# Sparse attention with an expert layer on one Trainium2 core: sixteen tiles normalised inside the turn, and a planner that counts TensorE's activity over a sliding stretch

## The chip, the cores and the metric

The kernel runs on one core of a Trainium2 chip. The metric is device time in microseconds (us). The kernel before takes 828.85 us, the median of 3 runs (826.21 to 830.17). The engines are named as the profile names them: PE is TensorE's matmul, PEld its weight load, DVE is VectorE, ACT is ScalarE, POOL is GpSimd, SP is the engine that issues most DMAs.

## The reference

```python
def _attn_ref(q, k, v):                    # (4, 8, 576, 64) each, float32
    scores = scale * np.matmul(q, k.transpose(0, 1, 3, 2))
    kth = np.partition(scores, -32, axis=-1)[..., -32:-31]
    scores = np.where(scores >= kth, scores, -1000000000.0)
    attn = np.exp(scores - np.max(scores, axis=-1, keepdims=True))
    attn = attn / (np.sum(attn, axis=-1, keepdims=True) + 1e-09)
    return np.matmul(attn, v)

def _moe_ref(x, w_a, w_b, w_out):          # x: (2304, 512), d_ff 1536
    return (x @ w_a) * (x @ w_b) @ w_out
```

Every row of attention keeps its 32 largest scores; the heads of a token are laid side by side and go through the expert layer. All is float32.

## The kernel before, in words

**The tiles.** The work is cut into 8 chunks of 256 or 320 tokens. A chunk has 4 pairs of heads, and a pair has 4 or 5 tiles: a tile is 64 query rows of both heads of a pair (128 partitions) against 576 keys. There are 144 tiles; tiles 0 to 15 are chunk 0, tiles 16 to 35 chunk 1. For each tile: `scores` (L456, TensorE) fills a PSUM tile; `topk` copies half of it out (L469 or L467, ACT), folds it into a minimum and a maximum half (L476, L478, DVE) and finds the 32nd largest score with four rounds of max8 and match_replace (L484, L486, DVE), with POOL making the exponent's bias (L489) for the first 36 tiles; `softmax` masks and exponentiates into P with the row's sum beside it. The first 35 tiles do this on TensorE and ACT: L520 (ACT) makes a mask, L525 (TensorE) adds it to the scores, L527 (ACT) is the exponential. Then L530 (POOL) adds 1e-9 to the sum, L533 (DVE) takes its reciprocal into `sm[:, 1:2]`, and L537 (POOL) multiplies the tile's P, 128x576, by it. `transpose` turns P in five blocks of 128x128 with TensorE transposes against an identity (L559), four into one PSUM tile `mm` and the fifth into another for the first 30 tiles, and ACT copies both out (L561). When all tiles of a pair are turned, `av` (L589) multiplies by V, and ACT and POOL split the result into a high and a low part (L599 to L601).

**The experts.** Weights come as float32 words and are converted into two fp32r parts by `convert` (L406 to L415: four ACT, one or two DVE and two POOL operations of 128x512 per weight, 36 weights, in the first 200 us), while attention of chunks 0 and 1 goes on. `up` (L627 to L629) and `down` (L661 to L663) are three fp32r products per block. For the first two chunks `up` also copies a second PSUM tile into the SBUF tile `b` (L648), and `down` copies its result into `b` before the store (L668). `b` has one buffer.

**The order of the work.** No engine's order is written by hand. Every operation is entered into `Plan` with an engine, a modelled cost, a key, what it reads and writes, and the buffers it needs. `Plan.order` then runs a model of the engines in time: a free engine takes the operation with the smallest key that is ready and whose buffers are free (a tag's buffers are taken in the order of the program; `mm` alone is free of that). The kernel is emitted in that order, and on the chip each engine works through its list strictly in order. Scores and top-k of tile i have the key -1000 + i, a tile's turn the key i, a chunk's experts 1000 and more, so that a turn gives way to later tiles' scores and goes ahead of the experts.

**TensorE's clock in the planner.** The model doubles the cost of a PE operation when the count of columns that ended in the last period of length `TICK` is under `BUSY`. Where PE has nothing for over `FILL_SLACK`, and the count of the present period is under `FILL_COLUMNS`, the planner puts in a filler: a bf16 product of 256 columns into an `mm` tile that nobody reads (L316). There are two `mm` buffers, shared by fillers, turned blocks of the first 30 tiles, one step of the first 24 conversions, `av`, `up` and `down`.

**DMA in the planner.** A load is modelled as landing 0.85 us after its bytes have passed; operations that read it are ready from then.

Of the kernel before, what the change touches and what calls it, by code (L numbers as in the profile page):

```python
# [8 lines left out]
FT = mybir.dt.float32  # L9
# [6 lines left out]
OP = mybir.AluOpType  # L16
# [9 lines left out]
KEEP = 1  # L26
APART = 24
FILL_SLACK = 0.15
XF_BUFS = 1
P_BUFS, JOINT = 2, 8  # L30
LAG = 0
# [7 lines left out]
MASKS = "P" * 35 + "QV" * 55  # L39
SCALAR_SCALE = 50  # L40
POOL_PRODUCT = 2
CONV_FIRST = 14
CONV_BIG = 4
CONV_AWAY = (0, 2, 4, 6, 8, 10, 11)
# [51 lines left out]
class Plan:  # L96
# [46 lines left out]
    def order(self):  # L143
        ops = self.ops
        n = len(ops)
        wait = [len(o.deps) for o in ops]
        outs = [[] for _ in ops]
        for k, o in enumerate(ops):
            for d in o.deps:
                outs[d].append(k)  # L150
        ready = [0.0] * n
        place = [0] * n
        for r, k in enumerate(sorted(range(n), key=lambda k: (ops[k].key, k))):
            place[k] = r
        held, head = {t: 0 for t in self.rings}, {t: 0 for t in self.rings}
        heaps, free = {e: [] for e in self.GAP}, {e: 0.0 for e in self.GAP}
        cols, events, drops, parked, taken, order = {}, [], [], {}, set(), []
        dma = hw = now = port = 0.0
        for k in range(n):
            if not wait[k]:  # L160
                heapq.heappush(heaps[ops[k].engine], (place[k], k))

        def wake(t):
            for r, k in parked.pop(t, ()):
                heapq.heappush(heaps[ops[k].engine], (r, k))

        def full(k):
            need = {}
            for b in ops[k].bufs:
                if b not in taken:  # L170
                    need.setdefault(b.tag, []).append(b)
            for t, bs in need.items():
                h = head[t]
                if held[t] + len(bs) > bs[0].bufs or t not in self.LOOSE and self.rings[t][h:h + len(bs)] != bs:
                    return t

        left, products = n, sum(o.engine == "PE" for o in ops)

        def fill():
            b = self.filler[0]()  # L180
            self.rings["mm"].append(b)
            b.left, b.first = 1, "PE"
            ops.append(Op("PE", self.filler[1], 0, lambda: self.filler[2](b), (), [b], 1, False, 0.65, False))
            outs.append([])
            return len(ops) - 1

        while left:
            started = False
            for e, h in heaps.items():
                if free[e] > now + self.EPS:  # L190
                    continue
                aside, pick = [], None
                while h:
                    r, k = heapq.heappop(h)
                    if ready[k] > now + self.EPS:
                        aside.append((r, k))
                        continue
                    t = full(k)
                    if t is None:
                        pick = k  # L200
                        break
                    parked.setdefault(t, []).append((r, k))
                for x in aside:
                    heapq.heappush(h, x)
                soon = min((ready[k] for _, k in aside), default=1e9)
                if pick is not None:
                    left -= 1
                    products -= e == "PE"
                elif (e == "PE" and products and now > FILL_FROM and now + FILL_SLACK < soon and held["mm"] < 2
                        and cols.get(int(now / self.TICK), 0) < FILL_COLUMNS):  # L210
                    pick = fill()
                else:
                    continue
                started = True
                order.append(pick)
                o = ops[pick]
                for b in o.bufs:
                    if b not in taken:
                        taken.add(b)
                        held[b.tag] += 1  # L220
                        head[b.tag] += 1
                        wake(b.tag)
                if e == "SP":
                    free[e] = now + 0.05 * o.num
                    hw = max(hw, now) + (0.625 if o.inner else 0.45) * o.num
                    dma = max(dma, hw + 0.65) + o.cost
                    end = dma + 0.85
                elif e == "PE":
                    slow = cols.get(int(now / self.TICK) - 1, 0) < self.BUSY
                    end = free[e] = now + o.cost * (2 if slow else 1)  # L230
                    tick = int(end / self.TICK)
                    cols[tick] = cols.get(tick, 0) + o.cost * 2400 * o.rows
                else:
                    end = now + o.cost
                    if o.port:
                        port = end = max(end, free["POOL"] + o.cost - self.SHARED)
                    elif e == "POOL":
                        end = max(end, port + o.cost - self.LOCKED)
                    free[e] = end
                heapq.heappush(events, (end, pick))  # L240
                heapq.heappush(events, (free[e], -1))
            if started:
                continue
            now = events[0][0]
            while drops and drops[0][0] <= now + self.EPS:
                t = heapq.heappop(drops)[1]
                held[t] -= 1
                wake(t)
            while events and events[0][0] <= now + self.EPS:
                end, k = heapq.heappop(events)  # L250
                if k < 0:
                    continue
                e = ops[k].engine
                for b in ops[k].bufs:
                    b.left -= 1
                    if not b.left:
                        at = end + (0 if e == b.first else self.HOP.get((e, b.first), 0.2))
                        heapq.heappush(drops, (at, b.tag))
                        heapq.heappush(events, (at, -1))
                for d in outs[k]:  # L260
                    wait[d] -= 1
                    to = ops[d].engine
                    ready[d] = max(ready[d], end + (self.GAP[e] if e == to else self.HOP.get((e, to), 0.2)))
                    if not wait[d]:
                        heapq.heappush(heaps[to], (place[d], d))
                        heapq.heappush(events, (ready[d], -1))
        self.length = now
        return order
# [10 lines left out]
def attn_moe(ctx: ExitStack, tc, qT, kT, kW, v, wa, wb, wo, out):  # L279
# [38 lines left out]
    def buf(shape, dtype, tag, bufs, pool=work):  # L318
        return Buf(pool, shape, dtype, tag, bufs)
# [179 lines left out]
    def softmax(i, s, found):  # L499
# [31 lines left out]
        else:  # L531
            act(1, lambda: nc.scalar.activation(sm[:, 1:2], sm[:, 0:1], AF.Copy, bias=1e-9), [], [sm], k=URGENT)
        dve(1, lambda: vec.reciprocal(sm[:, 1:2], sm[:, 1:2]), [], [sm])  # L533
        if i >= SCALAR_SCALE and i % 2 == 0:
            act(S, lambda: nc.scalar.activation(pt.ap, pt.ap, AF.Copy, scale=sm[:, 1:2]), [sm], [(both, w)], ptr=1)
        else:
            pool(0, lambda: nc.gpsimd.tensor_scalar(pt.ap, pt.ap, sm[:, 1:2], 1.0, op0=OP.mult, op1=OP.mult), [sm], [(both, w)], 0.81)  # L537
        return both

    PT = {}  # L540

    def transpose(i, both):
        t = tiles[i]
# [4 lines left out]
        for n, m in ((0, 4), (4, 5)) if i < FRONT else ((0, last),):  # L548
            tp = mm_tile() if i < FRONT else buf([128, 2, 512], FT, "tp", 1, psum)

            def at(tp=tp, n=n, m=m):
                x = tp.ap if i < FRONT else tp.ap.rearrange("p a b -> p (a b)")
                return x[:, 0:128 * (m - n)].rearrange("p (k q) -> p k q", q=128)

            def turn(at=at, n=n, m=m):
                pf = both.ap.rearrange("p w a b -> p (w a b)")
                of = [(640 if t["joint"] else S) * w + 128 * kb for kb in range(4)] + [512 if t["joint"] else S * w + 448]
                for kb in range(n, m):
                    nc.tensor.transpose(at()[:, kb - n, :], pf[:, of[kb]:of[kb] + 128], ident)  # L559
            pe((m - n) * 262, turn, [(both, w)] + ([(both, 0)] if t["joint"] and w else []), [tp])  # L560
            act(128 * (m - n), lambda at=at, n=n, m=m: nc.scalar.activation(  # L561
                turned[:, n:m, :, t["off"]:t["off"] + 64], at().rearrange("p k (h q) -> p k h q", h=2), AF.Copy),
                [tp], [(turned, t["s"], n)], ps=True, k=URGENT if i < FRONT and HURRY else None)
# [315 lines left out]
```

## Time and profile before

| | |
|---|---|
| median of 3 runs | 828.85 us |
| the profiled execution | 829.44 us |
| its span, first to last instruction | 827.7 us |
| mean granted clock of TensorE | 0.973 |
| busy share PE, DVE, ACT, POOL | 94%, 82%, 71%, 50% |

The profile is of one execution. The median is 0.6 us under its time, and 1.7 us of its time lie around the span. Busy shares are means over stages with different limits. PE's busy time counts fillers too, and modelled ends of pipelined matmuls, so a busy PE is not a useful one. The granted clock has two levels here, 1.2 GHz (0.5 in the profile's figures) and 2.4 GHz (1.0); a share between them is a mix of both over the stretch.

### The profile page before, as it was taken

The page shows a single profiled execution, that of the slowest core. Times are in us where ns is not written, and L with a number is a line of the kernel's source. Part 1 is how long each engine was busy: PE and PEld are TensorE (multiplying, and loading weights), DVE is VectorE, ACT ScalarE, POOL GpSimd, SP SyncE. Part 2 cuts the span into 40 slices and gives each one's busy share as a digit, 9 for nine tenths or more (in the row PEclk, how much of TensorE's full clock was granted, in tenths as well). Part 3 has the DMA queues.
Part 4 walks back from the last instruction along what each step waited for, and adds up shares of the span by engine and source line. Part 5 has one row for each costly group of instructions (what it writes and reads, how often), then busy time and mean ns, then how long its engine had stood idle before and what let it go on. Part 6 is the DMA issues. An engine that isn't in the chain of part 4 may idle for free. (4 is left out here: it accounts for less than half of the span.)

```text
span 827.7 us, 17219 instructions
## 1 busy us (share of the span) xinstructions
PE 782.1 (94%) x5736; PEld 611.0 (74%) x5736; DVE 680.7 (82%) x2239; ACT 584.2 (71%) x1348; POOL 412.6 (50%) x581
## 2 busy tenths in 40 slices
PE   5787879889999999999999999999999999999997
PEld 2333356765688876888778877887788878898995
DVE  6888998596999999999999999999999999960110
ACT  5888998997678777777677777777677767851220
POOL 3776887898376743444334443443344434440120
PEclk7788999989999999999999999999999999999999
DMA  7766767775277723776338834784367436650660
GB/s 259 270 233 238 252 227 247 284 249 172 71 219 249 237 91 113 260 253 213 101 109 272 294 139 143 273 294 127 128 227 259 155 105 223 215 199 26 208 238 29
DMA packets 76383, 163.46 MB, mean 197 GB/s; under 512 B 5888, under 2 KB 37632, under 8 KB 76288
## 3 DMA queue, kind: packets, MB, share of 16 engines
q1 hardware_dynamic: 76016, 162.03, 58.3%
q8 instruction: 48, 0.79, 0.4%
q14 instruction: 47, 0.39, 0.1%
q10 hardware_dynamic: 272, 0.26, 0.1%
HBM read 144.97 MB, written 17.30 MB: 196 GB/s over the span
## 5 line engine op out<-in xcount | busy, mean ns | idle before, releaser
L627 PE MATMUL mm<-xh,w 128*128 128x256 f32 (+1 forms) x768 | 240.5, 313 | 3.0 <-ACT pt L561 2.0
L629 PE MATMUL mm<-xh,w 128*128 128x256 f32 (+1 forms) x768 | 227.9, 297 | 0.0
L628 PE MATMUL mm<-xl,w 128*128 128x256 f32 (+1 forms) x768 | 227.9, 297 | 0.0
L484 DVE MAX8 top<-mx 128x8 f32<-128x296 f32 x432 | 186.7, 455 | 0.9
L627 PEld LDWEIGHTS mm<-xh,w 128*128 128x128 f32 x768 | 145.8, 190 | 19.4 <-issue 10.8
L628 PEld LDWEIGHTS mm<-xl,w 128*128 128x128 f32 x768 | 146.5, 191 | 0.3
L629 PEld LDWEIGHTS mm<-xh,w 128*128 128x128 f32 x768 | 145.8, 190 | 0.0
L651 POOL TENSOR_TENSOR gl<-a,gh 128x256 fp32r<-128x256 f32 (+1 forms) x96 | 79.3, 826 | 112.9 <-ACT gh L650 104.0
L486 DVE MATCH_REPLACE8 mx<-top,mx 128x296 f32<-128x296 f32 x288 | 128.6, 450 | 0.0
L510 POOL TENSOR_TENSOR p<-sb,p 128x576 f32<-128x576 f32 x55 | 78.2, 1422 | 73.8 <-ACT p L509 72.6
L561 ACT ACTIVATE pt<-tp 128x512 f32<-128x512 f32 (+1 forms) x114 | 74.6, 655 | 52.8 <-PE tp L559 51.7
L537 POOL TENSOR_SCALAR p<-p,sm 128x576 f32<-128x576 f32 x97 | 73.4, 757 | 63.1 <-DVE sm L533 63.0
L645 DVE SCALAR_TENSOR_TENSOR a<-mm,a 128x320 f32<-128x320 f32 (+1 forms) x72 | 32.9, 457 | 72.2 <-PE mm L629 68.2
L661 PE MATMUL mm<-wo,gh 128*128 128x512 f32 x216 | 89.0, 412 | 0.4 <-ACT pt L561 0.4
L663 PE MATMUL mm<-wo,gl 128*128 128x512 f32 x216 | 84.7, 392 | 0.0
L662 PE MATMUL mm<-wo,gh 128*128 128x512 f32 x216 | 84.5, 391 | 0.0
L589 PE MATMUL mm<-pt,vr 128*64 128x256 f32 (+1 forms) x544 | 77.1, 430 | 1.3 <-ACT pt L561 1.2
L559 PE MATMUL tp<-ident,p 128*128 128x128 f32 x522 | 77.6, 276 | 0.4 <-POOL p L537 0.4
L559 PEld LDWEIGHTS tp<-ident,p 128*128 128x128 f32 x522 | 60.2, 140 | 19.1 <-ACT bias L491 6.6
L650 ACT ACTIVATE gh<-a 128x256 fp32r<-128x256 f32 (+1 forms) x96 | 42.3, 441 | 41.9 <-DVE a L645 38.3
L476 DVE TENSOR_TENSOR mn<-s,sb 128x288 f32<-128x288 f32 x134 | 59.2, 445 | 14.2 <-ACT sb L469 12.6
L467 ACT ACTIVATE sb<-s 128x576 f32<-128x576 f32 x109 | 69.1, 635 | 1.2 <-PE s L456 1.2
(105 smaller groups left out, 1526.0 us busy)
## 6 DMA issues: line engine op xcount, KB each, us to landing
w<-wd SPq DMA_DIRECT2D x168, 512.0 KB, 4.4
wd<-w SPq DMA_DIRECT2D x24, 512.0 KB, 3.9
kr<-kT SPq DMA_DIRECT2D x32, 288.0 KB, 3.3
vr<-v SPq DMA_DIRECT2D x24, 384.0 KB, 3.6
kw<-kW SPq DMA_DIRECT2D x24, 288.0 KB, 3.6
wo<-wa SPq DMA_DIRECT2D x12, 512.0 KB, 5.9
qr<-qT SPq DMA_DIRECT2D x16, 320.0 KB, 5.0
wo<-wb SPq DMA_DIRECT2D x9, 512.0 KB, 5.3
```

The lines of the kernel that those rows point to most:

```text
L484: dve(HS + 8, lambda r=r: vec.max(eight(r), mx[:, g]), [(mx, g, 0), (mx, g, 1)], [tk[r]], 0.393)
L486: dve(HS + 8, lambda r=r: vec.match_replace(mx[:, g], eight(r), mx[:, g], LOW), [tk[r]], [(mx, g, 0), (mx, g, 1)], 0.453)
L510: pool(S, lambda: nc.gpsimd.tensor_tensor(pt.ap, sb.ap, pt.ap, OP.subtract), [sb], [(both, w)])
L559: nc.tensor.transpose(at()[:, kb - n, :], pf[:, of[kb]:of[kb] + 128], ident)
L589: mm(ps[e, :n], vr[:, (kb + 1) % 5, e], turned[:, kb, h, :n], start=(kb == 0), stop=(kb == 4))
L627: mm(ps[:, :n], w[:, 0, kb, :], xh[:, kb, :n], start=(kb == 0), stop=False)
L628: mm(ps[:, :n], w[:, 0, kb, :], xl[:, kb, :n], start=False, stop=False)
L629: mm(ps[:, :n], w[:, 1, kb, :], xh[:, kb, :n], start=False, stop=(kb == 3))
L651: pool(n, lambda: nc.gpsimd.tensor_tensor(gl[:, j, on], a[:, :n], gh[:, j, on].bitcast(FT), OP.subtract), [a, (gh, j)], [(gl, j)])
L661: mm(ps.ap, gh[:, j, on], fin[j][:, 0], start=(j == turn[c][0]), stop=False)
L662: mm(ps.ap, gh[:, j, on], fin[j][:, 1], start=False, stop=False)
L663: mm(ps.ap, gl[:, j, on], fin[j][:, 0], start=False, stop=(j == turn[c][-1]))
```

## The change

For tiles 0 to 15 the product of P with its rows' reciprocals leaves POOL. POOL instead scales the 128x128 identity by the reciprocals into a diagonal matrix (same instruction, 128 columns in place of 576), and each of the five blocks of P is turned by an ordinary float32 product with that diagonal in place of a transpose. The diagonal lies in a buffer of the tag `b`, of which there is one, so that the next tile's diagonal can be written only when the five blocks of the tile before have been turned.

The planner changes in three places. It counts columns over the last `TICK` before the present moment, in place of fixed periods, with the columns of an operation spread over its time. A filler is put in if that count is under `FILL_COLUMNS` where PE has nothing for `FILL_SLACK`, and also, where something becomes ready sooner, if the count is under `FILL_HOT`. A DMA is modelled as landing 1.5 us after its bytes have passed. So the emitted order can differ everywhere, on every engine and in the DMA queue.

```diff
+FILL_HOT = 4000
+LANDING = 1.5
+DIAGONAL = 16
@@ Plan.order
-        cols, events, drops, parked, taken, order = {}, [], [], {}, set(), []
+        recent, events, drops, parked, taken, order = [], [], [], {}, set(), []
+        def active():
+            while recent and recent[0][1] < now - self.TICK:
+                recent.pop(0)
+            return sum((end - max(start, now - self.TICK)) * rate for start, end, rate in recent)
-                elif (e == "PE" and products and now > FILL_FROM and now + FILL_SLACK < soon and held["mm"] < 2
-                        and cols.get(int(now / self.TICK), 0) < FILL_COLUMNS):
+                elif (e == "PE" and products and now > FILL_FROM and held["mm"] < 2
+                        and active() < (FILL_COLUMNS if now + FILL_SLACK < soon else FILL_HOT)):
                     pick = fill()
-                    end = dma + 0.85
+                    end = dma + LANDING
                 elif e == "PE":
-                    slow = cols.get(int(now / self.TICK) - 1, 0) < self.BUSY
-                    end = free[e] = now + o.cost * (2 if slow else 1)
-                    tick = int(end / self.TICK)
-                    cols[tick] = cols.get(tick, 0) + o.cost * 2400 * o.rows
+                    times = 2 if active() < self.BUSY else 1
+                    end = free[e] = now + o.cost * times
+                    recent.append((now, end, 2400 * o.rows / times))
@@ softmax
-        if i >= SCALAR_SCALE and i % 2 == 0:
+        if i < DIAGONAL:
+            one = diagonal[i] = buf([128, 512], FT, "b", 1)
+            pool(0, lambda: nc.gpsimd.tensor_scalar(one[:, 0:128], ident, sm[:, 1:2], 1.0, op0=OP.mult, op1=OP.mult), [sm], [one], 0.27)
+        elif i >= SCALAR_SCALE and i % 2 == 0:
@@ transpose
-                    nc.tensor.transpose(at()[:, kb - n, :], pf[:, of[kb]:of[kb] + 128], ident)
-            pe((m - n) * 262, turn, [(both, w)] + ([(both, 0)] if t["joint"] and w else []), [tp])
+                    if i < DIAGONAL:
+                        mm(at()[:, kb - n, :], pf[:, of[kb]:of[kb] + 128], diagonal[i][:, 0:128], start=True, stop=True)
+                    else:
+                        nc.tensor.transpose(at()[:, kb - n, :], pf[:, of[kb]:of[kb] + 128], ident)
+            pe((m - n) * (520 if i < DIAGONAL else 262), turn, [(both, w)] + ([(both, 0)] if t["joint"] and w else [])
+               + ([diagonal[i]] if i < DIAGONAL else []), [tp])
```

## Rows read from the trace of the kernel before

**Rows 1.** Busy time of each engine in four stretches, with granted clock and DMA share.

```profile
core 0: us, PE busy (x) PEld busy (x) DVE busy (x) ACT busy (x) POOL busy (x), PEclk, DMA share, GB/s
0.00:108.00 108.00, 80.72 (x478) 36.93 (x478) 88.39 (x274) 90.14 (x192) 73.06 (x107) 0.84 0.72 250
108.00:195.00 87.00, 76.40 (x555) 55.78 (x554) 69.59 (x209) 80.82 (x186) 74.40 (x105) 0.94 0.69 245
195.00:740.00 545.00, 543.22 (x4188) 444.89 (x4188) 516.81 (x1743) 397.76 (x937) 253.83 (x355) 1.00 0.58 191
740.00:828.00 88.00, 81.77 (x520) 73.39 (x518) 5.88 (x14) 15.48 (x35) 11.30 (x15) 0.99 0.35 124
```

**Rows 2.** What ACT waited for in 0 to 108: us in total, times, longest.

```profile
ACT wo L406 <- DMA wo<-wa: 3.9, 2, 2.5
ACT xf L599 <- PE mm L589: 3.4, 2, 1.8
ACT sb L469 <- PE s L456: 3.0, 1, 3.0
ACT pt L561 <- PE mm L559: 2.5, 4, 0.8
...
ACT mm L410 <- PE mm L316: 0.8, 2, 0.7
```

**Rows 3.** What DVE waited for in 0 to 108, the rows that name POOL.

```profile
DVE wo L412 <- POOL bias L489: 2.4, 1, 2.4
DVE sm L533 <- POOL sm L530: 1.5, 2, 1.2
```

**Rows 4.** Groups by line in 0 to 108: busy us, mean ns | idle before.

```profile
L316 PE MATMUL mm<-ident,nident 128*128 128x256 bf16 x132 | 31.8, 295 | 4.9 <-ACT pt L561 1.8 <-DVE wo L412 0.4
...
L559 PE MATMUL mm<-ident,p 128*128 128x128 f32 x80 | 16.2, 314 | 9.8 <-ACT pt L561 5.4 <-POOL sm L530 1.4 <-POOL p L537 0.7
L589 PE MATMUL mm<-pt,vr 128*64 128x256 f32 x80 | 13.6, 506 | 0.5 <-ACT pt L561 0.4
...
L537 POOL TENSOR_SCALAR p<-p,sm 128x576 f32<-128x576 f32 x16 | 12.0, 748 | 2.0 <-DVE sm L533 2.0
...
L489 POOL TENSOR_SCALAR bias<-t 128x1 f32<-128x1 f32 x18 | 3.8, 214 | 7.7 <-DVE t L484 7.2
...
L424 POOL TENSOR_SCALAR_AFFINE_SELECT ident<-ident 128x128 f32<-128x128 f32 x1 | 0.3, 292 | 0.1
```

**Rows 5.** Timeline of PE: turned blocks and one `av` at half and at full clock.

```profile
60.91 1.09 PE L559 MATMUL mm<-ident,p 128*128 128x128 f32 x4
...
63.52 4.53 PE L589 MATMUL mm<-pt,vr 128*64 128x256 f32 x20 [0.37 <-ACT pt L561]
...
91.54 0.74 PE L559 MATMUL mm<-ident,p 128*128 128x128 f32 x5 [0.29 <-ACT xf L599]
...
105.69 2.38 PE L589 MATMUL mm<-pt,vr 128*64 128x256 f32 x20
```

**Rows 6.** Busy time and granted clock inside the first 108 us, columns as in rows 1.

```profile
20.00:39.00 19.00, 14.47 (x78) 6.04 (x76) 16.43 (x48) 16.43 (x35) 14.87 (x21) 0.77 0.77 254
39.00:59.00 20.00, 15.86 (x98) 8.02 (x98) 15.39 (x48) 17.85 (x41) 14.91 (x22) 0.84 0.70 252
59.00:80.00 21.00, 16.82 (x98) 7.61 (x91) 18.09 (x61) 17.40 (x39) 15.03 (x23) 0.76 0.64 221
80.00:108.00 28.00, 22.61 (x160) 11.03 (x159) 26.39 (x84) 27.35 (x61) 21.36 (x31) 1.00 0.74 259
```

**Rows 7.** Timelines: tile 3's reciprocal, tile 2's fifth block; tile 6's, tile 5's.

```profile
36.13 0.15 DVE L533 RECIPROCAL sm<-sm 128x1 f32<-128x1 f32 x1
...
37.01 0.30 PE L559 MATMUL mm<-ident,p 128*128 128x128 f32 x1 [0.47 <-DVE gl L412]
...
54.73 0.15 DVE L533 RECIPROCAL sm<-sm 128x1 f32<-128x1 f32 x1
...
55.90 0.33 PE L559 MATMUL mm<-ident,p 128*128 128x128 f32 x1 [0.69 <-ACT pt L561]
```

More of the change, by code (lines that the diff above doesn't have):

```diff
@@ L538, in softmax @@
         return both
-    PT = {}
+    PT, diagonal = {}, {}
     def transpose(i, both):
```

## The prediction

> **What bounds the kernel now.** I read four views, from the whole to the part. First the busy time by stage [rows 1]. From 195 to 740 us PE is busy 543.2 of 545 us, and DVE 516.8; after that PE alone works off what is left. So from 195 us on the end is set by PE's remaining work, which the change leaves as it is: every tile from 16 on is turned as before, and no expert product changes. Before 195 us PE is not the bound. In 0 to 108, the time of chunk 0's attention, it is idle 27.3 us, and 31.8 us of its busy time are 132 fillers that nobody reads [rows 1, 4]. There the fullest engines are ACT (90.1 of 108) and DVE (88.4); POOL has 73.1. In 108 to 195 ACT has 80.8 of 87. All that the change adds or removes lies in the first 108 us, and chunk 0's experts and all later tiles stand behind it. So what the front gains or loses moves the end by about the same, and what does not reach ACT or DVE there costs nothing.
>
> Second, what these two wait for [rows 2, 3]. In 0 to 108 ACT waited 6.7 us for PE after its first tile (3.4 + 2.5 + 0.8), 3.9 for weights, and for POOL in no row; DVE waited 3.9 for POOL (2.4 + 1.5). Third, the groups of that stretch [rows 4] give the prices, and fourth the timeline [rows 5] the same PE work at both clock levels.
>
> The profiled execution took 829.4 us (span 827.7 and 1.7 around it), 0.6 over the median of 828.85; the sum is made against 829.4. A measurement of this kernel can tell about 0.5% from no change, 4.1 us, so "the same" is 824.7 to 833.0.
>
> **POOL's scaling goes.** It was 16 x 748 ns = 12.0 us [rows 4]. The diagonal is the same instruction on 128 columns. Between the same kind on 1 column (214 ns) and on 576 (748 ns) a line gives 214 + 127 x 534/575 = 332 ns; the nearest row of its very shape, another operation, has 292. I take 332: 16 x 332 = 5.3 us, and POOL has 6.7 us less to do. The ends are 7.3 us (at 292) and 0 (at 748). Little of this reaches the end. ACT waits for POOL in no row, and DVE for 3.9 us in two [rows 2, 3]. The rest of POOL's time is covered by ACT's and DVE's own work; without that cover the whole 6.7 would count. I take -1.0 us, as POOL's queue gets 9% shorter and the conversions ahead of those two small operations stay; ends -3.9 and 0.
>
> **The turn gets dearer on TensorE.** 80 transposes become 80 float32 products. The trace shows what a float32 product is: the four `av` of chunk 0 have 40 such products, and 80 matmuls stand in the row of L589 [rows 4], so two passes each. A pass of 256 columns at full clock in `av` takes about 2.38/20 = 0.12 us, with two running side by side in the array's halves; a turned block of 128 columns takes 1 pass, and five take 0.74 with a modelled end of the last near 0.27, so (0.74 - 0.27)/4 = 0.12 each. At half clock four take 1.09, the last near 0.47: 0.21 each [rows 5]. So I add one pass of 0.12 to 0.21 us per block, 9.4 us at full clock and 16.6 at half. The 27.3 idle us and the fillers of PE take it in. What is not covered is a delay in order: PE works through its list in order, so scores and masks behind a turn come 0.6 to 1.0 us later, and ACT's copies too. That counts only where ACT has nothing else, and ACT is idle 17.9 of 108 us [rows 1], 17%: 0.17 x 9.4 = +1.6 us. Ends 0 and +9.4 (each of the delays met in full, at full clock). Per tile POOL's part of the chain from reciprocal to turned block is 0.42 us shorter and PE's 0.6 longer, about even, so no gain is expected there.
>
> One rule speaks against the change. The Trainium skill (TensorE: Matmul & The Clock Gate, Terms) says that the transpose mode is 4 times faster for float32. By that, as an estimate, the 80 products would cost three more passes each, 28 us at full clock, and by the same 17% +4.8 us in place of +1.6, which would make the sum 829.5. The trace shows a factor of two: two passes where the transpose has one, of the same columns.
>
> **The clock.** From 20 to 80 us the granted clock is 0.77, 0.84 and 0.76 [rows 6], a mix of the two levels; 2 x (0.23 x 19 + 0.16 x 20 + 0.24 x 21) = 25 us of these 60 ran at 1.2 GHz. From 80 to 108 it is 1.00. In the slower stretches PE is busy 76 to 80% of the time, in the full one 81%; the shares lie too near each other to say from them what a few more fillers do. The change puts fillers in more evenly and more often, and the products are twice the columns in the turns. If the half clock went away, PE's work in ACT's 6.7 us of waits would halve, as `av` does (4.53 to 2.38): -3.4. I take half of that, -1.7. The ends are -3.4 and +3.4, for a plan whose fillers fall elsewhere and lose the full stretch too.
>
> **DMA and the new order.** Nothing is loaded more or less. The later modelled landing puts readers of weights further back in ACT's, PE's and POOL's lists, so that ACT meets fewer loads still under way; it waited 3.9 us for two [rows 2]. I take half, -2.0; ends -3.9 and +3.9, where a load has long landed and its reader stands behind other work. SP's list is planned by the same model, with the same transfers. The order as a whole is new from the first operation. That this is worth anything by itself no row shows; it gets 0, with the 6.2 us in which ACT was idle in 108 to 195 [rows 1] as its bound on either side.
>
> **The sum:** -1.0 + 1.6 - 1.7 - 2.0 = -3.1; 829.4 - 3.1 = 826.3, say **826.3 us**. All four terms at their better ends give -11.2 (818), at their worse +16.7 (846); the likeliest case by itself, with the terms about half out each way, is 822 to 833.
>
> **Rival 1: a front that runs at full clock and meets its loads (faster).** The fillers hold the clock from 20 us on and loads are met on time. ACT's waits for PE (6.7) and for weights (3.9) nearly vanish, 10.6, with DVE's 1.0 for POOL, less 1.6 for the longer turns: -10, so 819 us; half of it, 824, is already faster. For it: 25 us at half clock, in a stretch that holds nearly all fillers. Against it: 132 fillers did not hold it there, and ACT, busy 83% already, has own work to put in place of many waits. The Trainium skill (TensorE: Matmul & The Clock Gate, Part 4: PE-mode transpose) holds that transposes do not count as activity for the clock; by that rule the products of the change would count where the transposes did not. No row separates transposes from the rest: they are spread through the slow and the full stretches alike.
>
> **Rival 2: the one buffer of the diagonal (slower).** Tile i+1's diagonal may be written only when tile i's fifth block is turned, and that block waits in turn for one of two `mm` tiles. In the trace tile 3's reciprocal is there at 36.13 + 0.15, but tile 2's fifth block ends at 37.31; tile 6's at 54.88, tile 5's block at 56.23 [rows 7]. That is 1.0 and 1.4 us, and the five blocks now take 0.6 to 1.0 longer: about 2 us. If POOL stands at the diagonal in the order of its list, behind it wait the conversions' sums, the bias and the row sums of the next tiles, on which ACT's and DVE's exponentials and reciprocals hang. At half of the 15 handovers that is 15 us of POOL; with POOL's and its followers' slack taking half, +7 or 8, on top of the other terms' zero: 837 us. It decides if the chip's turns run later than the planner thinks, for the planner itself would put other POOL work ahead. Against it: reciprocals come some 6 us apart on the mean (16 in 108 us).
>
> **Rival 3: nothing to see.** If PE and POOL are both covered and the order neither gains nor loses, 829, inside the same band as the forecast.
>
> **Chances.** The forecast and rival 3 together, within 0.5%: 0.40. Rival 1 and what lies between it and the forecast: 0.38, since two of the four terms have their better ends far below the one I took and the stretch has 17.9 idle us on ACT to win. Rival 2, or an order that loses by PE's delays: 0.22. The range is to leave out 2 in 10: from 814, beyond rival 1 by part of the 6 us of ACT's second stretch, to 837, rival 2.
>
> **What would show it.** Right: in 0 to 108, or to wherever the fourth `av` then ends, POOL's scaling at 0.3 us in place of 0.75; 160 matmuls where 80 transposes stood; ACT's wait for weights shorter; the granted clock from 20 to 80 us above 0.85; the same work of PE from then on, and the point from which PE is full earlier by what the end gains. Rival 1: chunk 0's fourth `av` some 8 to 10 us earlier and a clock near 1.00 from 20 us on. Rival 2: POOL idle ahead of the diagonal with PE's turn as the releaser, and the fourth `av` later. Wrong altogether: a difference that arises after 195 us, such as PE idle between products or DVE with new waits.

## The result and the profile after

The changed kernel takes 819.86 us, the median of 6 runs (817.84 to 822.22), against 827.80 us (826.21 to 830.17, 6 runs) of the kernel before: the ratio is 0.990, with a 95% interval of 0.988 to 0.992. That is 7.9 us faster; the forecast was 826.3, inside "the same". The profiled execution, the slowest of the six, took 822.2 us and has a span of 820.5 us.

Busy time by stage of the kernel after, the stages cut 6 us earlier than in [rows 1] (us of the stage; then PE, PEld, DVE, ACT, POOL; granted clock; DMA share; GB/s):

```profile
0.00:102.00 102.00, 78.47 (x504) 43.91 (x504) 87.78 (x272) 87.92 (x187) 66.25 (x106) 0.87 0.74 255
102.00:189.00 87.00, 74.46 (x549) 54.75 (x548) 73.48 (x215) 79.28 (x185) 72.66 (x105) 0.94 0.73 251
189.00:734.00 545.00, 543.85 (x4200) 447.22 (x4199) 517.50 (x1741) 400.80 (x944) 258.12 (x356) 1.00 0.60 192
734.00:821.00 87.00, 80.37 (x509) 71.79 (x507) 5.59 (x13) 14.93 (x34) 10.69 (x15) 0.98 0.35 124
```

From the second stage on each one holds nearly the work of before, 6 us earlier; PE is again busy 543.9 of 545 us in the third. So the difference arises in the first stage. The timeline shows where it ends, in ACT's copy of the fourth `av` out of PSUM, with which chunk 0's attention ends but for the split into two parts; before:

```profile
108.24 0.45 ACT L599 ACTIVATE xf<-mm 128x256 f32<-128x256 f32 x1
```

and after:

```profile
102.65 0.36 ACT L613 ACTIVATE xf<-mm 128x256 f32<-128x256 f32 x1
```

5.6 us of the 7.2 between the two spans are there by that step. Groups by line of the kernel after in 0 to 102, against [rows 4]:

```profile
L570 PE MATMUL mm<-b,p 128*128 128x128 f32 x160 | 27.6, 314 | 5.7 <-POOL b L543 4.1 <-ACT pt L575 1.0 <-ACT xf L613 0.3
...
L323 PE MATMUL mm<-ident,nident 128*128 128x256 bf16 x80 | 20.6, 300 | 5.7 <-ACT pt L575 2.1 <-DVE wo L419 1.7
...
L543 POOL TENSOR_SCALAR b<-ident,sm 128x128 f32<-128x128 f32 x16 | 6.0, 377 | 7.0 <-PE mm L570 3.1 <-DVE sm L540 2.1 <-DVE mx L493 0.7
```

160 matmuls stand where 80 transposes stood, POOL's operation takes 377 ns in place of 748, and there are fewer fillers, 80 in this stretch in place of 132. What ACT waited for in 0 to 102, against [rows 2]:

```profile
ACT sb L476 <- PE s L463: 3.5, 1, 3.5
ACT pt L575 <- PE mm L570: 2.6, 5, 1.0
ACT xf L613 <- PE mm L603: 2.4, 3, 1.4
...
ACT wo L413 <- DMA wo<-wa: 1.4, 1, 1.4
```

Weights: 1.4 us in place of 3.9. PE: 2.6 + 2.4 = 5.0 in place of 6.7. And the granted clock inside the front, against [rows 6]:

```profile
20.00:39.00 19.00, 15.42 (x90) 8.61 (x87) 17.54 (x56) 18.46 (x41) 14.02 (x22) 0.76 0.73 259
39.00:59.00 20.00, 15.14 (x111) 9.13 (x112) 18.62 (x56) 19.35 (x43) 14.69 (x23) 0.93 0.78 270
59.00:80.00 21.00, 17.93 (x123) 10.49 (x122) 18.50 (x58) 19.06 (x42) 14.70 (x24) 0.90 0.77 260
80.00:108.00 28.00, 22.75 (x162) 12.28 (x158) 26.18 (x83) 25.69 (x57) 20.42 (x32) 0.94 0.70 235
```

By the forecast's formula 2 x (0.24 x 19 + 0.07 x 20 + 0.10 x 21) = 16 us of 20 to 80 ran at half clock, in place of 25, but 80 to 108 has lost 2 x 0.06 x 28 = 3 us. ACT and DVE are fuller from 20 to 59 us (37.8 and 36.2 us against 34.3 and 31.8).

### The profile page after: what moved, and what is told of

Read it like the earlier page. It is cut to its first block, busy times and chain, and to the rows that moved or that the text cites. A ratio compares the mean times of both kernels' runs of the same rounds, so it can differ in the third digit from the quotient of the medians.

```text
span 820.5 us, 17222 instructions
## 1 busy us (share of the span) xinstructions
PE 777.2 (95%) x5755; PEld 617.7 (75%) x5755; DVE 684.3 (83%) x2239; ACT 582.9 (71%) x1348; POOL 407.7 (50%) x581
## 4 chain that ended last, share of the span: by engine, by line
PE 82%; ACT 10%; POOL 3%; issue 1%; DVE 1%; DMA 1%; SPq 0%; ACTq 0%; POOLq 0%; DVEq 0%
PE mm L641 13%; PE mm L643 12%; PE mm L642 12%; PE s L463 8%; PE mm L603 8%; PE tp L572 7%; PE mm L675 6%; PE mm L677 6%; PE mm L676 6%; ACT p L534 2%; ACT pt L575 2%; PE mm L610 1%; PE mm L570 1%; ACT wo L413 1%; POOL wo L415 1%
## 5 line engine op out<-in xcount | busy, mean ns | idle before, releaser
L547 POOL TENSOR_SCALAR p<-p,sm 128x576 f32<-128x576 f32 x81 | 62.0, 766 | 69.5 <-DVE sm L540 69.0
L603 PE MATMUL mm<-pt,vr 128*64 128x256 f32 (+1 forms) x544 | 74.5, 418 | 0.9 <-ACT a L652 0.5
L463 PE MATMUL s<-kr,qr 64*64 64x288 f32 x688 | 62.2, 441 | 7.9 <-DMA qr<-qT 4.9
```

The source lines that it names most:

```text
L463: mm(s[rows, g, 0:HS], qr[on, h, t["off"]:t["off"] + 64], kr[on, h, :], start=True, stop=True)
L603: mm(ps[e, :n], vr[:, (kb + 1) % 5, e], turned[:, kb, h, :n], start=(kb == 0), stop=(kb == 4))
```

## The experiments

Each is compared with the kernel before in runs on the same chip; the ratio of the changed kernel itself is 0.990. In these comparisons the kernel before lies at 827.3 to 827.8 us, so medians from different ones can be set side by side to about half a us. An edit of an operation alone leaves the emitted order on every engine as it was (what is added or left out apart); an edit of the planner or of a modelled cost gives a new order.

**Each half alone.** First the planner without the diagonal, then the diagonal with the planner of before.

```diff
-DIAGONAL = 16
+DIAGONAL = 0
```

> The changed planner alone: no diagonal, POOL scales all of P and TensorE transposes as before; sliding count, more ready fillers and the later modelled landing stay. If the planner's order carries the gain (theory A, the forecast's reading: better clock, loads met on time, the diagonal about even), this is within 2 us of the changed kernel, 818 to 822. If the diagonal carries it (theory B: POOL's 6.7 us less and a shorter wait before the turn), it is back at 826 to 830. If it is the luck of one order among many (theory C), it lies anywhere from 815 to 833, and neither part alone tells.

Measured: 829.04 us, ratio 1.002 (1.001 to 1.004).

```diff
-        recent, events, drops, parked, taken, order = [], [], [], {}, set(), []
+        cols, events, drops, parked, taken, order = {}, [], [], {}, set(), []
...
-                    end = dma + LANDING
+                    end = dma + 0.85
...
```

> The diagonal alone, planned by the old planner (fixed periods, landing at 0.85 us, old rule for fillers). Theory A: 827 to 831, since POOL's relief (-1.0) and the longer turns (+1.6) are about even. Theory B: 818 to 822. Theory C: anywhere from 815 to 833, and the two single gains do not add up to 8 us.

Measured: 829.45 us, ratio 1.003 (1.001 to 1.005). Neither half gains by itself in these orders. Theories A and B fall in their plain form; the two effects do not add.

**The parts in a fixed order.** The changed kernel's order is kept. First POOL multiplies all of P again, besides making the diagonal.

```diff
+                nc.gpsimd.tensor_scalar(pt.ap, pt.ap, 1.0, 1.0, op0=OP.mult, op1=OP.mult)
                 nc.gpsimd.tensor_scalar(one[:, 0:128], ident, sm[:, 1:2], 1.0, op0=OP.mult, op1=OP.mult)
```

> The changed kernel in its own order on every engine, but for tiles 0 to 15 POOL also multiplies all of P by 1.0 in place just before it makes the diagonal, so that POOL's 12 us and their place in the chain to the turn are back while TensorE's products stay. If POOL's relief reaches the end (theory B), 4 to 8 us slower than the changed kernel, 824 to 828. If it is covered as forecast (theory A, -1.0), 820 to 822.

Measured: 826.24 us, ratio 0.999 (0.997 to 1.000), 6.4 us slower than the changed kernel. Its groups in 0 to 102:

```profile
L573 PE MATMUL mm<-b,p 128*128 128x128 f32 x152 | 26.8, 317 | 10.1 <-POOL b L545 8.4 <-ACT pt L578 0.8 <-DVE sm L540 0.4
...
L419 DVE SCALAR_TENSOR_TENSOR wo<-wo,mm 128x512 uint32<-128x512 uint32 x16 | 10.9, 682 | 4.3 <-POOL wo L415 2.6 <-ACT mm L417 1.6
L544 POOL TENSOR_SCALAR p<-p 128x576 f32<-128x576 f32 x16 | 10.8, 674 | 0.4
```

POOL's 10.8 us are back, and its followers wait: PE 8.4 us for the diagonals (4.1 in the changed kernel), DVE 2.6 for the conversions' sums (0.7 there). The fourth `av` comes 4.1 us later:

```profile
106.72 0.37 ACT L616 ACTIVATE xf<-mm 128x256 f32<-128x256 f32 x1
```

So in this order POOL's time is on the path. But the edit puts in 10.8 us on top of the diagonals' 6.0, where the change had taken out 12.0 - 6.0 = 6.0 us: 6.4 us is the price of more than was taken out, not the worth of the relief.

Then part of TensorE's products are transposes again:

```diff
-                    if i < DIAGONAL:
+                    if i < DIAGONAL and kb in (0, 4):
                         mm(at()[:, kb - n, :], pf[:, of[kb]:of[kb] + 128], diagonal[i][:, 0:128], start=True, stop=True)
```

> The changed kernel in its own order, but 64 of the 80 float32 products with the diagonal are transposes against the identity again, so these blocks of P stay without their rows' factor; the first and fifth block of each tile still wait for the diagonal. It takes 64 passes of 0.12 to 0.21 us off TensorE. Forecast (longer turns cost +1.6): 818 to 820, 1 us faster. If the products' activity holds the clock up: more half clock in the first 110 us and the same time or 2 to 4 us slower, 820 to 824.

Measured: 820.99 us, ratio 0.992 (0.990 to 0.995), which the runs can't tell from the changed kernel. The edit turns the three middle blocks of each tile back, so 48 of the 80 products and not 64; two matmuls for each of the 32 that stay, and one for each transpose, stand in its first stage:

```profile
0.00:101.00 101.00, 74.37 (x458) 37.59 (x458) 88.19 (x274) 88.28 (x188) 66.42 (x107) 0.85 0.75 258
```

```profile
L570 PE MATMUL mm<-b,p 128*128 128x128 f32 x64 | 16.4, 342 | 6.3 <-POOL b L543 3.6 <-ACT pt L575 1.6 <-ACT xf L613 0.3
...
L572 PE MATMUL mm<-ident,p 128*128 128x128 f32 x48 | 8.6, 292 | 0.0
```

PE is busy 4 us less, to no gain, and the clock is 0.85 against 0.87. All fillers still stand in this kernel, so it does not tell what the products alone do for the clock.

**The same exchange in the old order.** The kernel before, order and all, but with diagonals (in quarters of one buffer `b`) and products in tiles 0 to 15; the planner knows nothing of it. The edit is cut to its main lines.

```diff
+                    diagonal[i] = diagonal[-1][:, 128 * (i % 4):128 * (i % 4) + 128]
+                    nc.gpsimd.tensor_scalar(diagonal[i], ident, sm[:, 1:2], 1.0, op0=OP.mult, op1=OP.mult)
...
+                    if i < 16:
+                        mm(at()[:, kb - n, :], pf[:, of[kb]:of[kb] + 128], diagonal[i], start=True, stop=True)
```

> The order of the kernel before on every engine, but in tiles 0 to 15 POOL's scaling of P is replaced by the diagonal of 128 columns and TensorE's transposes by products with it; four diagonals fit (quarters of the buffer b), so no tile waits for the turn of the one before. Putting POOL's scaling back into the changed kernel's own order cost 6.4 us. If POOL's work in this stretch is worth that in any order (theory B), this is 820 to 823. If it is worth it only in an order that was planned with a short POOL operation (theory B', order and relief together), 826 to 829.

Measured: 829.28 us, ratio 1.002 (1.000 to 1.003). In this order the exchange as a whole is worth nothing, or costs 1.6 us. That fits B', but it does not show what POOL's relief alone is worth there, since TensorE's longer turns came with it unplanned. ACT's wait for turned blocks in 0 to 108 rose from 2.5 us in 4 waits [rows 2] to 7.7 in 13:

```profile
ACT pt L572 <- PE mm L568: 7.7, 13, 1.4
```

In the changed kernel, whose planner knew of the longer turns, it is 2.6. Relief without the longer turns was not run in the old order.

**How much is the draw of an order.** A draw is one order out of the many that the planner could write. Three kernels with the diagonal and the new planner that differ from the changed one in a number of the model. The first asks for the landing's part; the other two have no merit of their own.

```diff
-LANDING = 1.5
+LANDING = 0.85
```

> The changed kernel planned with a modelled landing of 0.85 us in place of 1.5; diagonal, sliding count and fillers stay. If the later landing is a needed part (loads met on time), 823 to 829 with more of ACT's time spent on weights still under way. If it is not, 818 to 822. Theory C (the luck of one order): anywhere from 815 to 833.

```diff
-            pool(0, lambda: nc.gpsimd.tensor_scalar(one[:, 0:128], ident, ...), [sm], [one], 0.27)
+            pool(0, lambda: nc.gpsimd.tensor_scalar(one[:, 0:128], ident, ...), [sm], [one], 0.30)
```

> The changed kernel planned with 0.30 us for the diagonal in place of 0.27, a change of the model by 0.03 us in 16 operations that has no merit of its own; it gives another order on every engine. If the gain belongs to the change as such, 818 to 822. Theory C: a spread of several us, 822 to 830 most likely, since two of two other new orders gave 829.

```diff
-LANDING = 1.5
+LANDING = 1.6
```

> The changed kernel planned with a modelled landing of 1.6 us in place of 1.5, a second change without a merit of its own that gives another order on every engine. Gain belongs to the change: 818 to 822. Theory C: 822 to 830.

Measured: 825.76 us with 0.85 (ratio 0.998, 0.996 to 0.999), 823.34 with 0.30 (0.995, 0.993 to 0.997), 825.15 with 1.6 (0.997, 0.995 to 0.999). With the changed kernel that makes four orders: 819.9, 823.3, 825.2, 825.8, mean 823.5. All four are faster than before; 0.03 us in a modelled cost is worth 3.5 us, and 0.1 us of landing in one direction costs about as much as 0.65 in the other (5.3 and 5.9). Then second draws for each half: the planner alone with a landing of 1.6, and the diagonal under the old planner with a cost of 0.30.

> The changed planner without the diagonal, planned with a landing of 1.6 us in place of 1.5: a second draw of an order for the planner alone, whose first was 829.0. If planner and diagonal are only worth something together, 826 to 831; if the first was a bad draw and the planner alone carries the gain, 821 to 825.

> The diagonal under the old planner, with 0.30 us in place of 0.27 as its modelled cost: a second draw for the diagonal alone, whose first was 829.5. Together only: 826 to 831. If the first was a bad draw and the diagonal carries the gain under either planner, 821 to 825, as with the new planner (819.9, 823.3, 825.2, 825.8).

Measured: 829.89 us (1.002, 1.001 to 1.004) and 839.90 us (1.016, 1.013 to 1.019). So the first draws were not unlucky ones: neither half gains in either of its two orders. In the slowest, DVE and ACT have a hole early, and the fourth `av` is 9.1 us behind that of the kernel before:

```profile
39.00:59.00 20.00, 16.39 (x99) 8.41 (x97) 12.21 (x38) 15.41 (x34) 11.18 (x18) 0.83 0.51 160
```

```profile
117.37 0.38 ACT L609 ACTIVATE xf<-mm 128x256 f32<-128x256 f32 x1
```

Its span is 838.3 us. In the traces of all fourteen kernels, the one before and the changed one among them, the fourth `av` comes at 100.7 to 117.4 us, and the span less that time lies between 714 and 721 us.

**The fillers.** The changed kernel's order with its 92 fillers left out of the program (operations numbered from `planned` on are fillers).

```diff
         for k in self.order():
+            if k >= planned:
+                continue
```

> The changed kernel in its own order on every engine with its 92 fillers left out of the program, so that only TensorE's own work holds the clock. So far the time did not follow the time at half clock (23.9 us of it before 200 us in a kernel of 829 us, 37.5 in the changed one). If the clock in the front is off the path, 818 to 822 though the half clock grows; if the forecast's term holds (ACT waits for slow turns and scores), 822 to 826.

Measured: 827.23 us, ratio 1.000 (0.998 to 1.002), 7.4 us slower than with them. The profile's clock has to be read with care here. By stage it says

```profile
20.00:39.00 19.00, 14.20 (x68) 8.65 (x71) 17.32 (x56) 17.27 (x38) 13.92 (x20) 1.00 0.70 245
...
80.00:108.00 28.00, 21.34 (x119) 13.20 (x120) 22.87 (x72) 22.89 (x50) 16.76 (x27) 0.64 0.53 187
```

but its timeline shows the scores of a tile, eight matmuls, at the longer duration until 40 us:

```profile
23.86 1.24 PE L466 MATMUL s<-kr,qr 64*64 64x288 f32 x8 [2.61 <-ACT p L537]
...
38.82 1.18 PE L466 MATMUL s<-kr,qr 64*64 64x288 f32 x8
...
45.75 0.72 PE L466 MATMUL tp<-kr,qr 64*64 64x288 f32 x8 [0.36 <-ACT p L537]
```

So PE stood at half clock to some 40 us, and again for 2 x 0.36 x 28 = 20 us after 80. ACT's wait for turned blocks grew from 2.6 to 7.2 us in the front:

```profile
ACT pt L578 <- PE mm L573: 7.2, 11, 1.6
```

The fourth `av` comes at 108.93 us, 6.3 us later. Nobody reads a filler, so what they are worth can hardly come by anything but the clock that they hold.

**The wait for the buffer.** The changed kernel's order, with the diagonals of four tiles side by side in `b`.

```diff
+            if i:
+                one.make = lambda: diagonal[0].ap
...
-            pool(0, lambda: nc.gpsimd.tensor_scalar(one[:, 0:128], ident, ...
+            pool(0, lambda: nc.gpsimd.tensor_scalar(one[:, quarter], ident, ...
...
```

> The changed kernel in its own order on every engine, but the diagonals of four tiles lie side by side in the buffer b, so that POOL no longer waits at a diagonal for the turn of the tile before (3.1 us in three waits in the changed kernel, with the releaser given as TensorE's product with the diagonal). If that wait (the slower rival) still costs something, 817 to 819; if it is covered, 819 to 821.

Measured: 820.40 us, ratio 0.992 (0.990 to 0.995), not to be told from the changed kernel. POOL's waits for PE at a diagonal are covered. No version beat the changed kernel.

## Why the prediction was right and where it was not

**Where the time lies: right.** PE's work from 195 us on is untouched and moved forward as a block; the front decides, and by the end of chunk 0's attention 5.6 us of the gain are there.

**The sum: right in sign, short in size.** 826.3 was forecast, 3.1 us under the profiled execution; measured was -7.9 between medians. Against the mean of the four orders (823.5, some 4 us under the kernel before) the sum was near, in part by luck, for single terms of it were off. Nor does the range of 814 to 837 tell much: of all kernels run here only the one at 839.9 lies outside it. The step that failed is "the order as a whole ... gets 0": the four orders lie 5.9 us apart, and the one at hand is the best of them, 3.7 us under their mean. The bound of 6.2 us beside that zero held.

**POOL, -1.0 with ends of -3.9 and 0: on the path, its size not isolated.** The diagonal took 377 ns and not 332, so POOL was spared 6.0 us and not 6.7. In the changed kernel's order 10.8 us put back cost 6.4; in proportion, as an estimate, 6.0 us are worth 3.6, near the better end. The -1.0 was read from the waits that name POOL in the old order, and those tell what POOL delays there, not what a planner makes of the time set free. In the old order the exchange gained nothing, but the longer turns were in it. That planner and diagonal gain only together is what the draws show, four orders with both against two with the planner alone and two with the diagonal alone. That it is POOL's freed time from which the new plan gains is argued: the conversions in the freed slots are a reading of the waits in the experiment that put POOL's scaling back, and no run took only these.

**TensorE's turn, +1.6 with ends of 0 and 9.4: the lower end, in an order planned for it.** Two passes per block are there; the timeline of the kernel after shows eight in 1.16 us at full clock, with a modelled end near 0.27 for the last, so 0.13 each:

```profile
25.78 1.16 PE L570 MATMUL mm<-b,p 128*128 128x128 f32 x8 [0.40 <-POOL b L543]
```

The trace does not bear out the factor of four that the Trainium skill gives (TensorE: Matmul & The Clock Gate, Terms): it is two. Taking 48 of the 80 products back gained nothing that the runs can tell, so PE's idle time covers them in a plan that counts them. In the old order, which did not, ACT's wait for turned blocks grew by 5.2 us (7.7 against 2.5).

**The clock, -1.7: about right in size, but not what orders the kernels.** Half clock between 20 and 80 us fell from 25 to 16 us; over the whole front it is some 35 us in place of 42, each with the first 8 us counted in, which the profile gives as 1.00 (last section): 2 x 0.13 x 102 = 27 and 2 x 0.16 x 108 = 35. In the fixed order of the changed kernel, leaving the fillers out cost 7.4 us through it: some 70 us at half clock in the front (40 at its start and, by the profile's 0.86 for 0 to 106, 2 x 0.14 x 106 = 30) in place of those 35, about 0.2 us for each; as an estimate, 7 us less would be -1.4. But kernels of different orders do not follow it: the diagonal alone had 0.91 in 0 to 108, against 0.84 before, and gained nothing; the one planned with 0.30 had 0.90 in its front and was 3.5 us slower than the one with 0.87.

Whether TensorE's transposes count as activity is not settled here. The Trainium skill holds that they do not count as busy in the same way (TensorE: Matmul & The Clock Gate, Part 4: PE-mode transpose). With 48 of the 80 products turned back into transposes the clock was 0.85 against 0.87 in the front, and 0.969 to 0.982 over the whole of six executions, against 0.973 to 0.987 in twelve with all products in that order (the changed kernel and the one with four diagonals). That leans the way of the rule, but passes are missing too, and the start that reads 1.00 though it ran at half clock is some 8 us long in the trace of the changed kernel and 20 in that of the four diagonals.

**DMA, -2.0: not shown.** ACT's wait for weights did fall by 2.5 us. But it is back at 3.9 with the landing of 0.85, at 4.2 (2.5 + 1.7) with the later one of 1.6, and these two are slower by 5.9 and 5.3 us; the one planned with the latest landing waited longest. The wait comes and goes with the draw.

**Rival 1** named the time, 819, and the kernel reached it by another way: full clock was not reached, and PE's waits fell by 1.7 us only. **Rival 2** was seen as a wait, 3.1 us at three handovers in place of half of fifteen, and cost nothing.

**Open:** the kernel before is itself one draw of its planner, and no neighbours of it were run. So how much of the mean gain of 4 us belongs to diagonal and planner, and how much to a poor draw before, is not settled beyond this: all four orders with both parts are faster than it, and the five kernels that lack one of them are not.

Nor is it settled what the diagonal adds to the new plan, POOL's time or TensorE's clock. In their traces the two kernels of the planner alone ran at half clock longer than any other that kept its fillers. The first stands at 0.88 in 0 to 108, which is 26 us, and at half clock for some 40 us more that the profile gives as 1.00 (last section):

```profile
0.00:108.00 108.00, 83.67 (x445) 37.02 (x446) 90.31 (x275) 88.97 (x188) 74.00 (x110) 0.88 0.72 250
```

The second has 0.84 there, 35 us, and some 27 us more (four transposes take 1.08 us at 19.52 and 0.66 at 27.82). So they have 66 and 62 us, against some 35 in the changed kernel, and at 0.2 us for each, an estimate from another order, that is 6 of the 9 us by which the first is slower than it and 5 of the 10 of the second. Against it stands that 48 transposes in place of products cost the changed order nothing that the runs can tell. No run held the clock for the planner alone.

## What to carry to other kernels

Where a planner writes the order, price a change as planned and as drawn: run two or three orders that differ in a meaningless number, and take their spread (here 6 us of 820) as the error of any single one before a part is given the credit. Waits in the old order tell what an engine delays there, not what its time is worth to a new plan: put the work back into the new order to see whether it is on the path, and put back as much as was taken out. Here work taken out of an order without a new plan gained nothing (48 passes of TensorE, POOL's waits at the diagonal), and work put in cost (10.8 us of POOL: 6.4 us).

## What the runs showed of the hardware

In these profiles the granted clock reads 1.00 up to the first change that is recorded, whatever it was: without fillers the first 39 us stand at 1.00 while the scores take 1.24 us there and 0.72 at full clock. In the changed kernel it is the first 8 us or so; its eight scores at 6.88 us take 1.18 us. The same holds for the planner alone, whose rows say 1.00 to 39 us:

```profile
20.00:39.00 19.00, 16.03 (x73) 7.36 (x73) 16.92 (x51) 16.90 (x38) 13.85 (x21) 1.00 0.69 250
```

```profile
32.76 1.24 PE L463 MATMUL s<-kr,qr 64*64 64x288 f32 x8
...
42.59 0.71 PE L463 MATMUL s<-kr,qr 64*64 64x288 f32 x8 [0.98 <-ACT p L534]
```

So a mean clock over a front can be compared between kernels only together with the durations at its start. Fillers that nobody reads were worth 7.4 us in the changed kernel's order, in a stretch where PE does not bound the kernel, and without them ACT's wait for turned blocks was 4.6 us longer (7.2 against 2.6).
